# ReLU-squared attention and a gated feed-forward on one core: planner's order replaced by a written-out one, transposes in 64x64 tiles, score tiles in any two PSUM banks

## The chip, the cores and the metric

The kernel runs on one core of one Trainium2 chip. The metric is the time of one execution in device microseconds (us). Below, PE is TensorE (the matrix engine), PEld its weight loads, DVE is VectorE, ACT is ScalarE, POOL is GpSimd, which here only issues loads, and SP is SyncE, which issues stores and the transposes done by DMA. PSUM, where TensorE writes, has eight banks in this kernel.

## The reference

```python
batch, n_heads, seq, head_dim = (8, 12, 448, 64)
scores = scale * np.matmul(q, k.transpose(0, 1, 3, 2))
attn = np.maximum(scores, 0.0) ** 2 / S
attn_out = np.matmul(attn, v)
x = attn_out.transpose(0, 2, 1, 3).reshape(B * S, H * D)   # 3584 x 768
gate = np.maximum(x @ w_gate, 0.0)      # w_gate, w_val: 768 x 1536
val = x @ w_val
out = gate * val @ w_out                # w_out: 1536 x 768
```

Scores are passed through a ReLU and squared; there is no softmax. All inputs and the output are float32; the matrix products run in bf16.

## The kernel before, in words

**Units of work.** Heads are taken in quads: a pair (b, g) is batch b (0 to 7) and four of its 12 heads (g is 0 to 2), so there are 24 quads. A sequence of 448 is seven tiles of 64 rows.

For each quad, query and key are loaded (converted to bf16 by the load) into one tile `raw` of 128 partitions, queries in partitions 0 to 63 and keys in 64 to 127 (lines 468 to 488), and turned, so that the head's dimension lies along the partitions, into `qkT`. The first six quads are turned on TensorE: the three of batch 0 by `transpose_first` (L540, L547) in two parts, three of seven query tiles first; the three of batch 1 by `transpose_pe` (L588). The other 18 go through a copy (`perm`, L610 and L612) and a DMA transpose on SP's queue (`transpose_dma`).

Attention of a quad is seven score steps, each of four matmuls in 64x64 tiles (L686) into two neighbouring banks that begin at an even bank (0-1, 2-3, 4-5, 6-7), a ReLU out of PSUM (L697 on ACT, L699 on DVE), and a square in place (L709 on ACT, L711 on DVE). In batch 0 it is done in two passes over the queries, 192 columns first and then 256, with up to two key tiles in a step, four steps to a pass. Then 28 matmuls in 64x64 tiles form the product with v ("PV", L728) in a pair of banks, and a copy (L744 on ACT, L746 on DVE) puts it into `xT`, the input of the feed-forward.

The feed-forward of batches 0 and 1 is plain (`gv_plain`, L793): six matmuls for a block of 128 columns of w_gate, six for w_val, a ReLU on ACT (L801), a product on DVE (L803). Batch 0's first six blocks are done in two parts of 192 and 256 columns. From batch 2 on, two batches at a time are multiplied by a seven-product scheme of Strassen's kind (`gv_strassen`, L902), and the output layer (`out_both`, L1017) likewise for every two batches; these need sums of weights that DVE makes once (L820 to L839), copies of partial products out of PSUM (`snapshot`, L849 to L855), and additions on DVE (L930 to L968, L1007).

**What sets the order.** Nothing is executed on creation: every piece is an `Op` with the engines that may run it, what it depends on, which buffers it takes (`alloc`) and which it reads. Three lists hold TensorE's operations (attention, and `ffn`), the operations of the other engines (`others`) and POOL's loads. `plan` (L244) then walks through modelled time: TensorE's two lines are merged by the string `PE_ORDER`, the loads by `LOAD_ORDER`, and every other operation is given to the engine on which it would end first, with a small lead or lag from the string `AHEAD`. The `Planner` (L64) holds the modelled times, picks the buffer that comes free first, and, up to a modelled 32 us, puts filler matmuls (L1171, on constant data, read by nobody) in where TensorE would idle. The order that results is fixed when the kernel is built: on the chip each engine runs its own queue in that order and waits at each instruction for what it depends on.

A transpose on TensorE is a matmul of the data with the identity. In `transpose_pe` one instruction takes 128 partitions (query and key tile together) into 64 output partitions, 28 for a quad:

```python
for j in range(2):
    for t in range(NT):
        for h2 in range(2):
            nc.tensor.transpose(ps_b[64 * h2:64 * h2 + 64, ps2.idx + j, t * 128:(t + 1) * 128],
                                st.raw()[:, 2 * j + h2, t, :], ident)
```

The page writes the tiling as 128*64 there, and as 64*64 at scores and PV.

Of the kernel before, what the change touches and what calls it, by code (L numbers as in the profile page):

```python
# [15 lines left out]
class Res:  # L16


    def __init__(self, n):
        self.free = {i: 0.0 for i in range(n)}  # L20
        self.by = {}

    def at(self, i):

        t, op = self.free[i], self.by.get(i)
        return t if op is None else max(t, op.end + Planner.LATE[1])


class Buf:


    def __init__(self, res, among=None, width=1):
        self.res, self.width = res, width
        self.among = among if among is not None else sorted(res.free)
        self.readers, self.last, self.idx = 0, 0.0, None

    def pick(self, now=0.0):

        best = None
        for i in self.among:  # L40
            if all(i + w in self.res.free for w in range(self.width)):
                t = max(self.res.at(i + w) for w in range(self.width))
                if best is None or max(t, now) < max(best[0], now):
                    best = (t, i)
        return best


class Op:


    def __init__(self, engs, emit, deps=(), alloc=(), reads=(), mode=None, grp=None):
        self.engs, self.emit = engs, emit
        self.deps, self.alloc, self.reads = list(deps), list(alloc), list(reads)
        self.mode, self.grp = mode, grp
# [4 lines left out]
        self.start = self.end = self.eng = None  # L59
        for b in self.reads:  # L60
            b.readers += 1


class Planner:  # L64
    NOUT = 8
    SWITCH = 0.1
    BIAS = 0.2
    MARGIN = 1.5
    LATE = (2.0, 1.0, 0.3)
    TO_LOAD, LOADED = 2.35, 0.95  # L70
    TO_TURN, TURNED, TURN = 1.7, 0.8, 3.65
    ISSUE = 0.28
    TO_HW = 1.9
    COLD = 4.6, 1.6
    FILL_FROM = 0.4
    FILL_COLD = 5.5
    FILL_UNTIL = 32.0
    FILL_MARGIN = 0.1
    GV_ORDER = '1256734'
    OUT_ORDER = 'ab1cd572364'  # L80
    END_ORDER = ('517364', '523')
    BUFFERS = (3, 11, 3, 4, 4, 4, 3)
    PV_PAIRS = (0, 0)
    JOIN = True
    TWO_QUEUES = True
    SPLIT = False
    MERGE = False
    URGENT = {'sh': -0.5, 'perm': 0.5}
    YIELD = {'sq': 0.1, 'sh': 0.1}
    PV_AT_0 = 0  # L90
    QT = 3
    PART = 6
    PV_AT = (1, 1)
    T_AT = (1, 1)
    MORE_UNTIL = 6
    BY_PE = 6
    ORDER = 'LV610ab2c3x4oy5rzqp'

    def __init__(self, banks):
        self.banks = banks  # L100
        self.t = {"POOL": 1.25, "DVE": 0.85, "ACT": 0.74, "SP": 0.74}
        self.ops = []
        self.mode = None
        self.dma_t = 0.0
        self.queues = [], []
        self.loads = []

    def free_at(self, bank):
        return self.banks.free.get(bank, 1e9)

    def now(self, op):
        return self.t.get("PE", 0.0) if "PE" in op.engs else 0.0

    def ready(self, op):
        r = 0.0
        for d in op.deps:
            if d.end is None:
                return None
            if d.eng != "PE" or "PE" not in op.engs:
                r = max(r, d.end + (self.LATE[0] if d.xbar else self.LATE[2] if d.load else 0.0))  # L120
        for b in op.alloc:
            p = b.pick(self.now(op))
            if p is None:
                return None
            r = max(r, p[0])
        return r

    def best(self, op):
        r = self.ready(op)
        if r is None:  # L130
            return None
        c = None
        for e, (occ, busy) in op.engs.items():
            if e in ("DVE", "ACT"):
                r = max([r] + [d.end + self.MARGIN for d in op.deps if d.load and not d.hw])
            s = max(r, self.t.get(e, 0.0))
            if e == "PE" and op.mode != self.mode:
                s = max(r, self.t.get(e, 0.0) + self.SWITCH)
            f = s + busy + (self.BIAS if e == "DVE" and len(op.engs) > 1 else 0.0)
            if c is None or f < c[0]:  # L140
                c = (f, s, e)
        return c[1], c[2], r

    def rates(self, a, b):

        if not (a and b):
            return 1.0, 1.0
        share = a[0][0].share
        return 1.0 - share, share

    def flow(self, a, b, t, until):
        while t < until and (a or b):
            rates = self.rates(a, b)
            d = min([q[0][1] / r for q, r in zip((a, b), rates) if q] + [until - t])
            t += d
            for q, r, post in zip((a, b), rates, (self.LOADED, self.TURNED)):
                if q:
                    q[0][1] -= d * r
                    if q[0][1] < 1e-6:
                        q.pop(0)[0].end = t + post  # L160
        return t

    def transfer(self, queue, op, arrival, work):


        self.dma_t = max(self.flow(*self.queues, self.dma_t, arrival), arrival, self.dma_t)
        self.queues[queue].append([op, work])
        self.flow(*([list(x) for x in q] for q in self.queues), self.dma_t, 1e9)

    def commit(self, op, s, e):  # L170
        assert op.behind is None or op.behind.start is not None
        op.start, op.eng = s, e
        occ, busy = op.engs[e]
        if e == "PE" and s < self.COLD[0] and op.kind != "fill":
            occ, busy = occ * self.COLD[1], busy * self.COLD[1]
        now = self.now(op)
        self.t[e] = s + occ
        op.end = s + busy
        if e == "PE":
            self.mode = op.mode  # L180
        if op.hw:
            self.transfer(0, op, s + self.TO_HW, op.load)
        elif op.load:
            self.loads.append(op)
            self.transfer(0, op, s + (op.to or self.TO_LOAD), op.load)
        elif op.xbar:
            self.transfer(1, op, s + self.TO_TURN, self.TURN)
        else:
            op.end += op.land
        for b in op.alloc:  # L190
            t, b.idx = b.pick(now)
            assert t <= s + 1e-6
            for w in range(b.width):
                del b.res.free[b.idx + w]
                b.res.by.pop(b.idx + w, None)
            b.last = op.end
        for b in op.reads:
            b.readers -= 1
            b.last = max(b.last, op.end + (self.LATE[1] if op.land or op.xbar else 0.0))
            if b.readers == 0:  # L200
                for w in range(b.width):
                    b.res.free[b.idx + w] = b.last
                    if op.xbar:
                        b.res.by[b.idx + w] = op
        self.ops.append(op)
# [3 lines left out]
PE_ORDER = (  # L209
    'aaaccdabaabcbdafjabbaebbbaacdfhafcBBADDaabbabgaZLBKMBAccabaGCFFFCFFdagbaJJebjHHbbaAEFaadEcaaGBCBAAggcbaAFLDGFA'  # L210
    'PGGbaaCCCACgfcccBEbbaGEEDACedcccCCbbaDAfgAbbacBDCaaAAAhccbCCbaBCAaAadBeAabacBJbaDBACBDGcBFAAFAACBHAAGBAFBBCBAA'
    'BDfaAADaaCCAAcBBABaaABBAacbabDAGDAEABBCAIEAEACABAAcACbaAACAGAabbBABaaBCADAecbEACAaAFebaBACEAabEEFAfaBFgaCAabdA'
    'CbbaGBAdeCBecdCAaaaAAAABaebaAEKADBAQCBADADABAAAbaDBAbbBDAAACacFBAaabFBACCGCCABcbaCDBAADEbbaEABCAIBBAdIAAbdHFAA'
    'CaaDACCCaJACBABCBBfbaBABaccAACADbaAAAAadaaICAcaAAaaABAaabaBBbaaCEIACaFKBAAJABBAACABAAABCBBBACBCDCBAABAAAADADHC'
    'BDCBICHABCFBHACAFEBEHBABCAEGBBDBBDCCECAAAGBABBABBBCGEAABBCBCCBABBABBBA'
)
LOAD_ORDER = (
    'aaaaaafcbaakaacaaedbbbthbcabkacccefhbdiggaggaacddaaeebfdbecaccacabfdebcgagbaaeabhabddeaacejejafacacaammkbddbbf'
    'dacabba'
)  # L220
AHEAD = (
    'llmmmmmokormnnqmompmmmhjklmmnmipkpololmiqoqmkllqqmomnhllolkigjnnliqpkqgqhhhpoogrknspsnhshlookqpdonnfpqionrfqtn'
    'vnquafpyepllvskpmjquaslaoutinvmhcfqgyorlobnoqtvjgjlhcelpookkqilpkbselllhiclmsvapkwpqjjrogngkwmkmdcanruprtcgmtj'
    'srnqgtsopdunjkjkdkjrmrkrjnnrwisoqkkiknlllnqknpqrknfjokmiolpnfsxqlpdjnmglirqjjpnpkiiiloilpjpqosmionomrknpneelrm'
# [19 lines left out]
def plan(first, att, ffn, others, pool, still, filler, banks):  # L244
# [5 lines left out]
    pe = []  # L250
# [1034 lines left out]
```

## Time and profile before

| | |
|---|---|
| runs of the kernel, us | 402.48, 404.31, 405.04 |
| median, us | 404.31 |
| span of the profiled execution, us | 402.3 |
| granted TensorE clock, mean | 0.990 |
| DVE / ACT / POOL busy, us | 326.1 / 274.0 / 75.7 |
| first feed-forward matmul (L793) starts, us | 27.53 |
| last matmul's end (L1017), us | 398.2 |

The page gives no time of the profiled execution other than its span. "Span" runs from the first instruction to the last. A row such as `0.50 PE ps L686 x8` in the chain says that eight matmuls of line 686, writing `ps`, took 0.50 us of the chain of work that ended last. In the table of windows, the columns are the window, its length, the busy us and instructions of PE, PEld, DVE, ACT and POOL, the granted clock (1.00 is full), the share of the DMA engines (which goes over 1 where packets overlap) and GB/s. A timeline row gives start, length from first start to last end, engine, line, operation, tile written and read, tiling, shape and number, and the idle time ahead.

### The profile page before, as it was taken

The page shows a single profiled execution, that of the slowest core. Times are in us where ns is not written, and L with a number is a line of the kernel's source. Part 1 is how long each engine was busy: PE and PEld are TensorE (multiplying, and loading weights), DVE is VectorE, ACT ScalarE, POOL GpSimd, SP SyncE. Part 2 cuts the span into 40 slices and gives each one's busy share as a digit, 9 for nine tenths or more (in the row PEclk, how much of TensorE's full clock was granted, in tenths as well). Part 3 has the DMA queues.
Part 4 walks back from the last instruction along what each step waited for, and adds up shares of the span by engine and source line. Part 5 has one row for each costly group of instructions (what it writes and reads, how often), then busy time and mean ns, then how long its engine had stood idle before and what let it go on. Part 6 is the DMA issues. An engine that isn't in the chain of part 4 may idle for free.

```text
span 402.3 us, 8737 instructions
## 1 busy us (share of the span) xinstructions
PE 393.8 (98%) x3472; PEld 210.1 (52%) x3472; DVE 326.1 (81%) x568; ACT 274.0 (68%) x399; POOL 75.7 (19%) x121
## 2 busy tenths in 40 slices
PE   6999999999999999999999999999999999999995
PEld 3567745454455554444455554444555555555563
DVE  5688788999989879969988989888789967758662
ACT  3697786477979728969879868878788843333221
POOL 7946441020430110311030221300100000000000
PEclk9799999999999999999999999999999999999999
DMA  8999999948988995193698796682224320000245
GB/s 121 192 198 199 201 193 183 147 48 136 124 144 171 162 116 115 26 145 56 84 141 153 152 131 129 82 92 47 46 37 99 80 59 2 0 0 2 59 118 139
DMA packets 77337, 43.54 MB, mean 108 GB/s; under 512 B 40688, under 2 KB 77296, under 8 KB 77296
## 3 DMA queue, kind: packets, MB, share of 16 engines
q0 software_dynamic: 34640, 23.50, 43.1%
q1 hardware_dynamic: 42192, 18.98, 26.5%
q8 instruction: 27, 0.44, 0.5%
q10 hardware_dynamic: 464, 0.49, 0.4%
q14 instruction: 14, 0.11, 0.1%
HBM read 47.19 MB, written 11.01 MB: 145 GB/s over the span
## 4 chain that ended last, share of the span: by engine, by line
PE 95%; DMA 1%; DVE 1%; POOL 0%; issue 0%; ACT 0%; POOLq 0%
PE ps L902 36%; PE ps L1017 25%; PE ps L793 14%; PE ps L686 10%; PE ps L728 8%; DMA gvT<-in_q_dram 1%; PE ps L1171 1%; PE ps L540 1%; PE ps L588 1%; DVE at L711 1%; POOL gvT L404 0%; DVE at L699 0%; DVE qkT L515 0%; DVE f L853 0%; ACT xT L744 0%
## 5 line engine op out<-in xcount | busy, mean ns | idle before, releaser
L697 ACT ACTIVATE at<-ps 128x896 bf16<-128x896 f32 (+4 forms) x116 | 103.2, 906 | 22.6 <-PE ps L686 21.8
L849 ACT COPY f<-ps 128x448 f32<-128x448 f32 x99 | 52.1, 532 | 45.8 <-PE ps L902 34.2
L709 ACT ACTIVATE at<-at 128x896 bf16<-128x896 bf16 (+1 forms) x72 | 67.0, 947 | 2.0 <-DVE at L699 1.2
L711 DVE TENSOR_TENSOR at<-at 128x896 bf16<-128x896 bf16 (+4 forms) x99 | 58.9, 607 | 9.2 <-ACT at L697 8.1
L699 DVE TENSOR_SCALAR at<-ps 128x896 bf16<-128x896 f32 (+4 forms) x55 | 58.4, 1064 | 6.9 <-PE ps L686 6.2
L404 POOL DMA_DIRECT2D vv<-in_v_dram x44 | 26.7, 611 | 165.5 <-PE ps L686 152.5
L686 PE MATMUL ps<-qkT 64*64 64x448 bf16 (+2 forms) x756 | 51.5, 342 | 1.0 <-ACT xT L744 0.3
L902 PE MATMUL ps<-xT,gvT 128*128 128x448 bf16 x216 | 50.9, 353 | 0.0
L902 PE MATMUL ps<-sx,wv 128*128 128x448 bf16 x216 | 50.6, 353 | 0.1
L902 PE MATMUL ps<-xT,wg 128*128 128x448 bf16 x216 | 49.7, 353 | 0.0
L902 PEld LDWEIGHTS <-gvT 128*128 128x128 bf16 x324 | 30.7, 98 | 30.5 <-issue 3.2
L1017 PEld LDWEIGHTS <-sh 128*128 128x128 bf16 x312 | 29.5, 98 | 22.9 <-issue 3.6
L1017 PEld LDWEIGHTS <-hT 128*128 128x128 bf16 x270 | 25.3, 98 | 20.5 <-issue 4.5
L1017 PE MATMUL ps<-wo,hT 128*128 128x384 bf16 x192 | 35.6, 327 | 0.0
L686 PEld LDWEIGHTS <-qkT 64*64 64x64 bf16 x756 | 19.5, 106 | 27.5 <-issue 22.4
L728 PE MATMUL ps<-at,vv 64*64 64x448 bf16 (+2 forms) x700 | 33.4, 327 | 0.0
L1007 DVE SCALAR_TENSOR_TENSOR o<-ps,f 128x384 f32<-128x384 f32 x41 | 22.5, 554 | 12.1 <-PE ps L1017 7.2
L902 PEld LDWEIGHTS <-wv 128*128 128x128 bf16 x216 | 20.6, 98 | 21.0 <-issue 2.8
L793 PE MATMUL ps<-xT,wv 128*128 128x448 bf16 (+2 forms) x180 | 31.3, 316 | 0.0
L902 PEld LDWEIGHTS <-wg 128*128 128x128 bf16 x216 | 20.6, 98 | 19.9 <-issue 1.7
L851 ACT ACTIVATE f<-ps 128x384 f32<-128x384 f32 x37 | 18.2, 491 | 18.6 <-PE ps L1017 18.3
L793 PE MATMUL ps<-xT,wg 128*128 128x448 bf16 (+2 forms) x180 | 30.6, 315 | 0.0
(72 smaller groups left out, 495.5 us busy)
## 6 DMA issues: line engine op xcount, KB each, us to landing
out_dram<-o SPq DMA_DIRECT2D x108, 96.0 KB, 2.2
vv<-in_v_dram POOLq DMA_DIRECT2D x44, 112.0 KB, 5.1
raw<-in_k_dram POOLq DMA_DIRECT2D x18, 224.0 KB, 5.4
raw<-in_q_dram POOLq DMA_DIRECT2D x18, 224.0 KB, 6.0
wo<-in_moe_w_out_dram POOLq DMA_DIRECT2D x4, 576.0 KB, 16.7
wg<-in_moe_w_gate_dram POOLq DMA_DIRECT2D x5, 384.0 KB, 9.9
wv<-in_moe_w_val_dram POOLq DMA_DIRECT2D x5, 384.0 KB, 10.6
gvT<-in_k_dram POOLq DMA_DIRECT2D x5, 224.0 KB, 6.3
```

Of the source, the lines that this page charges most:

```text
L404: op = Op({"POOL": (0.5 + 0.0004 * n_desc,) * 2}, lambda: nc.gpsimd.dma_start(out=dst(), in_=src), deps=deps, alloc=alloc)
L686: nc.tensor.matmul(banks()[64 * j:64 * j + 64, z, h2], lhsT=self.k_of(j, h2, k), rhs=self.q_of(j, h2), start=True, stop=True)
L697: nc.scalar.activation(self.at_of(i, m), banks(), AF.Relu)
L699: nc.vector.tensor_scalar_max(self.at_of(i, m), banks(), 0.0)
L709: nc.scalar.activation(a, a, AF.Square)
L711: nc.vector.tensor_tensor(a, a, a, ALU.mult)
L728: nc.tensor.matmul(ps[64 * h2:64 * h2 + 64, ps2.idx + j, :n], lhsT=st.v_of(j, h2, c), rhs=self.at_of(c)[64 * j:64 * j + 64, 0, h2], start= ...
L793: nc.tensor.matmul(ps[:, pb.idx, z * n:(z + 1) * n], lhsT=w[:, kd, fc], rhs=xT_t[xbuf[b].idx][:, kd, cols], start=(kd == 0), stop=(kd == K ...
L849: nc.scalar.copy(dst, src)
L902: nc.tensor.matmul(ps[:, pb.idx, :S], lhsT=w(g)[:, fc], rhs=rhs, start=start and g == 0, stop=stop and g == KH - 1, skip_group_check=True)
L1007: op = Op({"DVE": V384}, lambda: nc.vector.scalar_tensor_tensor(o_t[ob.idx], ps[:, pb.idx, :OH], float(out_scale), f_t[fb.idx][:, :OH], AL ...
L1017: nc.tensor.matmul(ps[:, pb.idx, :OH], lhsT=lhs(kf), rhs=rhs(kf), start=start and kf == 0, stop=kf == FH - 1, skip_group_check=True)
```

## The change

The planner, its constants and its three strings go. In their place stands one string, `PLAN`, and a function `replay` that reads it: for each operation a number (two characters to the base 64, in the order of the lists passed at the end of the kernel), its engine if it may run on more than one, and the number of every buffer it takes; the number 4095 stands for filler, with bank, count and width.

```diff
+PLAN = (
+    '9r9p9nQ19o++7B6OQ2Q3Q5Q4QA09t9qQ80000Q7021++64609u0Q69s039w1012QB++536G9v00B3400D7020A613A31++235GA700451Q9A'
...
+)
+def replay(ops, filler):
+    text = iter(PLAN)
+    def number(n=1):
+        v = 0
+        for _ in range(n):
+            v = 64 * v + DIGITS.index(next(text))
+        return v
...
+        i = number(2)
...
+        if i == FILL:
+            filler(number(), number(), number(2))
+            continue
+        op = ops[i]
+        op.eng = list(op.engs)[number() if len(op.engs) > 1 else 0]
         for b in op.alloc:
+            b.idx = (number(), number()) if b.apart else number()
+        op.emit()
...
-    for op in plan(first, att, ffn, others, pool_ops, still_op, filler, r_ps):
-        op.emit()
+    replay([*sum(first, []), *att, *[o for o, _ in ffn], *others, *pool_ops], filler)
```

A pair of banks for scores or PV may now be any two; reads and writes step from one to the other:

```diff
-        return Buf(r_ps, among if among is not None else PAIRS, width=2)
+        return Buf(r_ps, width=2, apart=True)
+    def both(pair, src=None):
+        i, j = sorted(pair.idx)
+        return (ps if src is None else src)[:, i:j + 1:j - i, :]
```

All transposes on TensorE take 64x64 tiles, a query tile (a = 0) and a key tile (a = 1) each by itself and into a bank of its own. In `transpose_pe` that is 56 instructions, a alternating:

```diff
+    def turn(bank_of, st, a, slots, js=(0, 1), shift=0):
+        for t in slots:
+            for j in js:
+                for h2 in range(2):
+                    pb, c = bank_of(a, j)
+                    nc.tensor.transpose(ps_b[64 * h2:64 * h2 + 64, pb.idx, c + (t - shift) * P2:c + (t - shift + 1) * P2],
+                                        st.raw()[64 * a:64 * a + 64, 2 * j + h2, t, :],
+                                        ident[64 * a:64 * a + 64, 64 * a:64 * a + 64])
...
         def emit():
-            for j in range(2):
-                for t in range(NT):
-                    for h2 in range(2):
-                        nc.tensor.transpose(ps_b[64 * h2:64 * h2 + 64, ps2.idx + j, t * 128:(t + 1) * 128],
-                                            st.raw()[:, 2 * j + h2, t, :], ident)
+            for t in range(NT):
+                for a in range(2):
+                    turn(lambda a, j: (pbs[a], j * S), st, a, (t,))
```

In `transpose_first` a quad's keys are turned by two operations of 14 instructions, each with its own copy of 448 columns; they wait for the keys alone. Its early queries are turned by one operation of 12 (for the first quad two of 6), with one copy of 384 columns, and its late queries by one of 16 with a copy of 512, as before. Before, an early operation turned keys and queries together, with copies of 384 or 640 columns.

What `PLAN` holds of the start, in the order of each queue (S a score step, "b g / first column . step"; K, Q, L the turns of keys, early and late queries; fill as count x columns):

```
PE   fill 11x408; K00.0; Q00.0; fill 4x384; Q00.1; K00.1; fill 3x400; S00/0.1 .3 .0; fill 3x336; K01.0;
     fill 5x376; K02.0; S00/0.2; K01.1; Q01; K02.1; fill 3x304; S01/0.3 .0 .2; fill 5x408; Q02; S01/0.1; L00;
     fill 2x440; S02/0.3 .1; PV00/0; S02/0.0 .2; L01; S00/192.3; fill 2x320; S00/192.2; L02; PV01/0;
     S02/192.3; S00/192.0 .1; PV02/0; S02/192.1; S01/192.0; gate 0, 3; fill 2x416; gate 1; S01/192.2; PV00/192;
     S02/192.2 .0; value 0, 1; S01/192.1 .3; value 3; gate 2; value 2; turn 10; PV02/192; PV01/192; S10.5 ...
ACT  Q00 copy; ReLU 00/0.1 .0; K01.0; ReLU 00/0.2; K02.1; ReLU 01/0.3 .2; square 01/0.3; ReLU 01/0.1; L00;
     ReLU 02/0.3; xT 00; ReLU 02/0.2 .0, 00/192.2 .3, 02/192.3, 00/192.0; xT 02; ReLU 02/192.1; gate 0;
     ReLU 01/192.0; gate 3, 1; ReLU 01/192.2, 02/192.2 .0, 01/192.3 .1; gate 2; square 01/192.3 ...
DVE  ... ReLU 01/0.0; square 01/0.0; Q02; squares 01/0.2 .1; ReLU 02/0.1; squares 02/0.3 .1 .2; L01; L02;
     square 02/0.0; xT 01; ReLU 00/192.1 ...
POOL keys 00 (two loads), 01, 02; early q 01; v 00; late q 01, 00; early q 02; v 00; late q 02; v 02;
     w_gate 0; v 02, 01, 01; w_val 0; w_gate 2-3; w_gate 1; w_val 1; w_val 2-3; q 10; k 10; w_gate 4-5 ...
```

In POOL's queue before, early query 01 stood ahead of keys 02.

More of the change, by code (lines that the diff above doesn't have):

```diff
@@ L19, in __init__ @@
     def __init__(self, n):
[L20 to L26, printed above, removed]
-class Buf:
[L32 to L45, printed above, removed]
+        self.n = n
+class Buf:
+    def __init__(self, res, width=1, apart=False):
+        self.res, self.width, self.apart = res, width, apart
+        self.idx = None
 class Op:
-    def __init__(self, engs, emit, deps=(), alloc=(), reads=(), mode=None, grp=None):
+    def __init__(self, engs, emit, deps=(), alloc=(), reads=(), mode=None):
         self.engs, self.emit = engs, emit
         self.deps, self.alloc, self.reads = list(deps), list(alloc), list(reads)
-        self.mode, self.grp = mode, grp
+        self.mode = mode
         self.load = self.land = self.share = 0.0
@@ L58, in __init__ @@
         self.xbar = 0
[L59 to L120, printed above, removed]
-        for b in op.alloc:
[L122 to L205, printed above, removed]
@@ new lines, in replay @@
+def replay(ops, filler):
[5 more added lines that the diff above has]
+        return v
+    left = set(range(len(ops)))
+    while True:
+        try:
+            i = number(2)
+        except StopIteration:
+            break
+        if i == FILL:
+            filler(number(), number(), number(2))
+            continue
+        left.remove(i)
+        op = ops[i]
+        op.eng = list(op.engs)[number() if len(op.engs) > 1 else 0]
+        for b in op.alloc:
+            b.idx = (number(), number()) if b.apart else number()
+        op.emit()
+    assert not left
@@ new lines, in transpose_first @@
+        for j in range(2):
+            deps = [st.k_ops[j] if two else st.k_ops[0], id_op] + keys[-1:]
+            keys.append(pe(lambda j=j: turn(lambda a, j: (kb[j], 0), st, 1, range(NT), (j,)), 0.22,
+                           deps=deps, alloc=[kb[j]] + ([st.qt_buf] if j == 0 else []), mode="64x64"))
+        cps = [copy_qk(keys[j], kb[j], lambda j=j: qkT_t[st.qt_buf.idx][:, 1, j, :], lambda j=j: ps_b[:, kb[j].idx, :S], K448)
+               for j in range(2)]
+        if two:
+            qs = []
+            for j in range(2):
+                qs.append(pe(lambda j=j: turn(lambda a, j: (qb, j * HALF), st, 0, range(QT), (j,)), 0.095,
+                             deps=[st.q_ops[j], id_op] + (keys[:1] if j == 0 else qs), alloc=[qb] if j == 0 else [], mode="64x64"))
+        else:
+            qs = [pe(lambda: turn(lambda a, j: (qb, j * HALF), st, 0, range(QT)), 0.19, deps=st.q_ops + [id_op, keys[0]],
+                     alloc=[qb], mode="64x64")]
@@ L575, in rest @@
             return op
-        return ops, rest
+        return [*keys, *qs], rest
     def transpose_pe(b, g):
@@ L643, in __init__ @@
             m = 512 // n
-            starts = [*range(0, QT, m), *range(QT, NT, m)] if (b, g, c0) == (0, 0, 0) else range(0, NT, m)
+            starts = range(0, NT, m)
             ends = [*starts[1:], NT]
@@ L1012, in evac_add, with out_mm @@
         return op
-    def out_mm(lhs, rhs, pb, start, deps, seg, alloc=(), reads=(), grp=None):
+    def out_mm(lhs, rhs, pb, start, deps, seg, alloc=(), reads=()):
         def emit():
@@ L1074, in out_both @@
         rest = None
-        if Planner.JOIN and b == B - 4:
+        if b == B - 4:
             keep()
@@ L1160, with filler @@
     others.extend([still_op, id_op])
-    def filler(us, cold):
-        pb = bank([7, 6, 5, 4, 3, 2, 1, 0])
-        total = int(us * (1200 if cold else 2400))
-        n = (total + S - 1) // S
-        width = max(64, total // n)
-        def emit():
-            for _ in range(n):
-                nc.tensor.matmul(ps[:, pb.idx, :width], lhsT=still[:, :128], rhs=still[:, :width], start=True, stop=True)
-        op = Op({"PE": (us, us)}, emit, deps=[still_op], alloc=[pb], reads=[pb])
-        op.kind = "fill"
-        return op
+    def filler(bank, n, width):
+        for _ in range(n):
+            nc.tensor.matmul(ps[:, bank, :width], lhsT=still[:, :128], rhs=still[:, :width], start=True, stop=True)
     for g in range(NQ):
```

336 lines of the change are left out of this document (135 added, 201 removed).

## The prediction

> **What bounds the kernel now.** I read the page first, then the chain that ended last in order of time, then the windows of the first 30 us, then the timeline of TensorE. The page:
>
> ```profile
> span 402.3 us, 8737 instructions
> PE 393.8 (98%) x3472; PEld 210.1 (52%) x3472; DVE 326.1 (81%) x568; ACT 274.0 (68%) x399; POOL 75.7 (19%) x121
> ...
> PE   6999999999999999999999999999999999999995
> ...
> PE 95%; DMA 1%; DVE 1%; POOL 0%; issue 0%; ACT 0%; POOLq 0%
> ```
>
> TensorE is busy in every slice but the first and the last, so what counts is what it is busy with. The chain shows it:
>
> ```profile
> 21.05 1.67 PE ps L1171 x9
> ...
> 27.60 2.58 PE ps L793 x30
> ...
> 30.63 0.90 PE ps L588 x28
> 31.53 1.75 PE ps L728 x56
> 33.30 0.59 ACT xT L744
> 33.94 4.75 PE ps L793 x42
> ...
> 155.00 0.50 PE ps L686 x8
> ...
> 239.41 0.64 DVE f L853
> ...
> 398.20 0.56 DVE o L1007
> ```
>
> L1171 is filler that nobody reads. The first feed-forward product (L793) starts only at 27.53 (27.60 in the chain); from there to 398.2, 370.6 us, TensorE works almost without a gap: the waits in the chain are 0.59 at 33.30 and 0.64 at 239.41. In that stretch only useful columns and turns between tilings cost time. A pure score step of 8 matmuls takes 0.50 where 8 x 448 columns in four tiles are 0.37, and six output matmuls take 1.08 after a score step against 0.97 elsewhere, so each visit to 64x64 tiles costs 0.13 + 0.11 = 0.24 us; there are 64 visits after 27.5, 15 us. The start is another matter:
>
> ```profile
> 9.00:12.00 3.00, 2.94 (x44) 1.70 (x44) 1.35 (x4) 1.87 (x3) 2.59 (x5) 0.50 1.38 189
> 12.00:15.00 3.00, 3.00 (x47) 1.75 (x44) 1.87 (x4) 1.21 (x2) 3.00 (x5) 0.50 1.32 199
> 18.00:21.00 3.00, 2.66 (x101) 2.04 (x94) 2.97 (x7) 2.92 (x6) 3.00 (x5) 1.00 1.62 190
> ```
>
> From 9 to 15 TensorE is "busy" at a granted clock of 0.50, on filler and transposes, while ACT is busy 3.08 of 6; from 18 on DVE (2.97 of 3) and ACT (2.92) are full. So the start is limited by how early ScalarE and VectorE get their score tiles.
>
> **The part that the plan settles.** The profiled span is 402.3, 0.2 below the fastest of the three runs and 2.0 below their median, 404.31; the page has no time outside the span, so I make the sum on the span and carry the 2.0. Decoding PLAN (two characters an operation, then engine and buffers) gives 1782 operations and 10 fills. Products, their columns and the score matmuls are those of before; 65 visits to 64x64 tiles follow the first product, against 64. So after the start the plan neither adds nor removes TensorE work: +0.24 at most.
>
> What moves is the start. Ahead of the first product, PLAN has the three first score passes with their PV and 7 of the 12 steps of the second pass; before had 24 score matmuls and one PV of the second pass more behind it, and spent time on filler at 20.98, 23.35, 24.83 and 26.76. I follow the queue that ends last, ScalarE's.
> (1) The second quad's query load is now one place later on POOL (a 224 KB key load goes ahead). It landed at 8.92; 224 KB at 189 GB/s is 1.2 us, so 10.1. Turn (0.2), VectorE copies (0.4 + 0.36), scores and key copies on ScalarE: ReLU from about 12.0.
> (2) From there ScalarE has, to the last xT copy: ReLU 4 x 0.81, 2 x 0.49, 2 x 1.03, 2 x 0.60, one square 0.47 (estimate, half of the 768 row's 0.85), one key/query copy 0.57 (estimate between 0.48 for 384 and 0.90 for 896 columns), 2 xT copies x 0.48: 9.5 us. First product at 21.6 if it is never starved.
> (3) On to the last square that PV needs: 6 x 1.03 + 0.60 ReLU, 4 gate ReLU x 0.33, one square 0.60: 8.7, to 30.2, then one PV of 28 x 256 columns, 0.75: 30.9.
> (4) TensorE alone from 21.6 to there: 8 short products x 0.52 (2.58/5), fill 0.35, 36 score matmuls 0.96, 3 PV 2.24, one turn 0.47, three visits 0.72: 8.9, to 30.5. It is no longer than ScalarE.
> (5) VectorE from 12.0 to its last square before the first PV copy: 2 x 0.96 + 6 x 0.55 + 0.35 + 3 copies 1.2: 6.8, to 18.8; it is not the last.
> At that point the new order has three short products more than before had at 33.94 (1.55) and three score steps less (0.69): it stands where before stood at 34.8. Unstarved, the gain is 34.8 - 30.9 = 3.9. In 18 to 30 before, ScalarE was busy 11.08 of 12 us (92%); at that share the 18.2 us take 19.7 and the point is at 32.4: gain 2.4. I take the middle, **-3.2**, as the new list alternates as tightly as the old one.
>
> Weights and loads: 17 loads stand ahead of and with the first value weights. In destination bytes 2496 KB have to flow; the windows had let 2.2 MB through by 15 us and 2.8 by 18, so they flow by 17 and land 1.6 later, as the query load did (754 KB had flowed at 7.3): 18.6, before 21.6. The block that the third product needs comes at 21.6: TensorE may wait some tenths there, and the fill before it covers that. If loads slip by 1 us, so does the start.
>
> **The turns.** 28 transposes of 128x64 (L588) become 56 of 64x64. The nearest rows:
>
> ```profile
> 16.96 0.69 PE L547 MATMUL ps<-ident,gvT 64*64 64x64 bf16 x32 [0.41 <-DVE at L699]
> 30.56 0.97 PE L588 MATMUL ps<-ident,gvT 128*64 128x128 bf16 x28
> ```
>
> The first row is in two column tiles of one row half: (0.69 - 0.19 for the last one's length) / 32 = 15.6 ns each. With both row halves alternating, as `turn` is called, columns would share four ways: 56 x 7.8 = 0.44. If the pitch of 15.6 is a floor per instruction, 56 take 0.87 and nothing is won on 0.90. Scores in four tiles do run at a quarter of their columns (28 PV matmuls 1.32 us), so I take 0.47: -0.43 each, one of three already counted, **-0.86**.
>
> TensorE: Matmul & The Clock Gate (the Trainium skill, section "Wait — 56ns, not 53.3ns?") says that start-to-start never drops below about 25 ns however short a matmul. By that, an estimate, 56 turns would take 1.4 us and the three cost 2.8 more than in my sum, 403.0. The trace's 15.6 ns in tiles is against it.
>
> **Smaller parts.** First turns: keys apart from queries, 14 + 14 + 12 + 16 turns a quad; at 15.6 ns 0.9, against 1.53 (at half clock) + 0.25; they lie beside the ReLU queue, counted in (1), and if that cover goes they gain. Copies at the start: two of 640 and one of 512 (1.40) become two of 448, one of 384, one of 512 (0.39 x 2 + 0.36 + 0.42 = 1.56): counted in the queues. Pairs of banks apart: 138 of 171 score tiles and 18 of 27 PV tiles are no old pair. No row shows an eviction over banks apart; from below, nothing is won after 30 us, where no wait of TensorE on a bank is shown, and at most the 0.8 us of such waits ahead of it; from above, as much as two single copies against one wide one (2 x 0.53 - 0.92 = 0.15 us), on engines with 19% and 32% idle. I take 0. Engines: ReLU 130 on ACT and 41 on DVE (116 and 55), squares 103 on DVE (99), 26 copies of partial products move to DVE (13): by the rows ACT loses about 6 us and DVE gains 3; neither fills. SP keeps stores and DMA transposes in one queue as before; the end is the same last product, addition (0.56) and store, 4.1 us. POOL's loads after the start wait on buffers as before (24 us the longest), hidden. The 0.64 wait at 239 goes; I let one of its size take its place. Sum: -3.2 - 0.86 = -4.1; 404.3 - 4.1 = **400.2**, span 398.2.
>
> **Rivals.**
> B, better: ScalarE never starved (-3.9), no wait in the middle (-0.64), turns -0.86: -5.4, 398.9. Against it: the 92%. For it: the list is free to put any ready eviction next. 0.20.
> C, the clock halves again. Before, it fell at 9 after a window with TensorE busy 1.75 of 3.00; the fills between 9 and 18 (17 matmuls, 6,352 columns, 2.6 us) would last twice as long; part hides under ScalarE, so between +0.9 (the one fill of 5 x 408 right ahead of scores) and +2.6: 402.0. For it: key loads still land at about 9. Against: new fills stand at 5 to 9. 0.12.
> D, a turn has a floor that the number of active tiles doesn't lower: at 15.6 ns nothing is won in three turns, +1.2: 401.4. For it: no row shows a shorter pitch. Against: the scores' and PV's four-way sharing. 0.15. TensorE: Matmul & The Clock Gate (the Trainium skill) has such a floor, as told above.
> E, the other side: the middle. Every score visit is preceded by an eviction in a fixed order; if VectorE is late by the 0.64 of the row at 239, TensorE waits, as nothing overtakes. Seven such waits use up 4.1 us; at 13 of the 65 visits, 8.3 us, 408.5. For it: DVE at 81%, with slices of 9. Against: only one such wait in 370 us of a like order. 0.08.
>
> **How the numbers follow.** The forecast, 0.45 (own range 399 to 401.6), is the likeliest. About 1% (4.0 us, 400.27) is what a measurement tells from no change. Half of the forecast and all of B lie below, 0.22 + 0.20, and C or D with a start as in B, 0.05: faster 0.47. Slower than 408.35 is half of E, 0.04, and C, D and part of E together, 0.01: 0.05. The rest, 0.48, is the same. Range: B's 398.9 with its queue 0.9 earlier, 398.0, to C with D's, 403.2; outside lie E and the edges.
>
> **What would show it.** First product near 22 instead of 27.53; ReLU from 12.0; the state of 34.8 at 30.9 to 32.4; turns of 56 in 0.44 to 0.6 us; granted clock 1.00 from 9 to 15; no wait over 0.7 after 35; the end 4.1 after the last matmul. It is wrong if the first product is after 25, or if TensorE's waits after 35 add to over 2 us.

## The result and the profile after

| | before | after |
|---|---|---|
| median of the compared runs, us | 403.97 (402.48 to 405.04, 4 runs) | 503.77 (501.47 to 507.35, 4 runs) |
| span of the profiled execution, us | 402.3 | 505.5 |
| granted TensorE clock, mean | 0.990 | 0.939 |
| first feed-forward product starts, us | 27.53 | 33.40 |

The ratio is 1.2485 (95% interval 1.2417 to 1.2554). The forecast was 400.2, and 398.0 to 403.2. Slower by over 1% had a chance of 0.05, on the strength of rival E, which ended at 408.5. So the sign, the size and the place were all missed, and both signs of being wrong that the prediction named have come: the first product is after 25, and TensorE's waits after 35 us add to far over 2 us.

Here and below, a run over 1.5% above the fastest of its kernel is counted among the runs but left out of the ratios and their intervals.

The page after, in the same lines as before:

```profile
span 505.5 us, 8969 instructions
PE 424.9 (84%) x3598; PEld 221.2 (44%) x3598; DVE 330.8 (65%) x581; ACT 271.9 (54%) x388; POOL 75.5 (15%) x121
...
PE   7767688995888869988866799868798989999996
...
PE 72%; ACT 14%; DVE 9%; DMA 2%; issue 2%; DVEq 0%; SPq 0%; ACTq 0%
```

ScalarE and VectorE do about the work of before (ACT 271.9 against 274.0, DVE 330.8 against 326.1), so their instructions got no dearer; the engines stand still more. TensorE is out of work for 505.5 - 424.9 = 80.6 us, before 8.5: that is 72 of the 103 us. The other 31 are TensorE's own busy time (424.9 against 393.8): by the lower clock 393.8 would become 415 (x 0.990 / 0.939, an estimate), and some 10 I can't assign. The row of 40 slices tells where: holes throughout, except in the last six slices. From 428.5 on no attention is left, and TensorE has no wait at all in that stretch.

What it waits for stands in the list of TensorE's waits, of which these are some (line waited in, who released it; us in total, times, longest). Before, the same list has none after 35 us.

```profile
PE ps L721 <- ACT at L516: 16.2, 16, 2.6
PE ps L506 <- ACT at L516: 16.1, 18, 2.2
PE ps L612 <- ACT at L516: 9.6, 8, 2.2
PE ps L506 <- DVE at L518: 6.3, 6, 2.1
PE ps L836 <- ACT at L516: 5.6, 6, 1.4
```

L516 and L518 are the ReLUs that empty a pair of score banks; L506 is the scores; L721, L612 and L836 are products of the feed-forward, each into one bank of its own. Some waits of a product on a ReLU are due, when it takes over a bank from it. But the list for all engines holds waits between instructions that share no data: an eviction (a copy or ReLU out of PSUM) on an eviction by the other engine, or a ReLU on a product of the feed-forward.

```profile
DVE at L518 <- ACT at L516: 14.9, 9, 3.7
...
ACT at L516 <- DVE at L518: 11.4, 6, 3.7
...
ACT at L516 <- PE ps L721: 10.2, 11, 2.1
```

One place shows the mechanism. Here is the timeline of TensorE and ScalarE from 243.6 to 248 us (start, length, engine, line; in brackets the idle time ahead and what ended it):

```profile
243.63 0.76 PE L506 MATMUL ps<-qkT 64*64 64x448 bf16 x12
...
244.23 0.92 ACT L516 ACTIVATE at<-ps 128x896 bf16<-128x896 f32 x1 [1.10 <-PE ps L506]
...
245.20 0.73 PE L721 MATMUL ps<-sx,wv 128*128 128x448 bf16 x3 [0.81 <-ACT at L516]
245.77 0.73 PE L721 MATMUL ps<-xT,gvT 128*128 128x448 bf16 x3
245.97 0.92 ACT L516 ACTIVATE at<-ps 128x896 bf16<-128x896 f32 x1 [0.82 <-PE ps L721]
...
246.94 1.30 PE L721 MATMUL ps<-xT,wg 128*128 128x448 bf16 x6 [0.44 <-ACT at L516]
```

Decoding PLAN for this place gives the banks. The three score steps write banks 4 and 1, 2 and 7, 5 and 0. The first ReLU reads 1 and 4. The product at 245.20 adds into bank 3, which this ReLU doesn't touch but which lies between 1 and 4, and it starts when the ReLU has ended (244.23 + 0.92 = 245.15). The second ReLU reads 2 and 7; ScalarE has been free since 245.15, and waits until the product in bank 3 is done (245.20 + 0.73 = 245.93). The product at 245.77 goes into bank 1, outside of 2 to 7, and runs beside this ReLU. The two products at 246.94 go into banks 4 and 2 and wait for its end (246.89); of these two only bank 2 is one that it reads.

This gives **theory 1**: a read that steps over banks, `ps[:, i:j + 1:j - i, :]`, is ordered against everything in the banks between, not only against its own two. 139 of the 198 pairs in PLAN are not neighbours. **Theory 2**: the written-out order is so tight that any delay spreads. **Theory 3**: the low clock at the start (0.80 up to 35 us) and the turns cost it.

### The profile page after: what moved, and what is told of

It reads as the page before. It is cut to its first block, busy times and chain, and to the rows that moved or that the text cites. A ratio compares the mean times of both kernels' runs of the same rounds, so it can differ in the third digit from the quotient of the medians.

```text
span 505.5 us, 8969 instructions
## 1 busy us (share of the span) xinstructions
PE 424.9 (84%) x3598; PEld 221.2 (44%) x3598; DVE 330.8 (65%) x581; ACT 271.9 (54%) x388; POOL 75.5 (15%) x121
## 3 DMA queue, kind: packets, MB, share of 16 engines
q1 hardware_dynamic: 42192, 18.98, 21.6%
## 4 chain that ended last, share of the span: by engine, by line
PE 72%; ACT 14%; DVE 9%; DMA 2%; issue 2%; DVEq 0%; SPq 0%; ACTq 0%
PE ps L721 27%; PE ps L836 17%; PE ps L612 12%; ACT at L516 12%; PE ps L506 7%; PE ps L547 6%; DVE at L518 4%; PE ps L981 2%; ACT xT L563 2%; DMA out_dram<-o 1%; PE ps L359 1%; DMA raw<-in_k_dram 1%; DVE xT L565 1%; DVE f L672 1%; DVE sh L919 1%
## 5 line engine op out<-in xcount | busy, mean ns | idle before, releaser
L516 ACT ACTIVATE at<-ps 128x896 bf16<-128x896 f32 (+4 forms) x130 | 116.0, 903 | 92.8 <-PE ps L506 20.2
L506 PE MATMUL ps<-qkT 64*64 64x448 bf16 (+2 forms) x756 | 57.6, 356 | 30.0 <-ACT at L516 16.1
L530 DVE TENSOR_TENSOR at<-at 128x896 bf16<-128x896 bf16 (+3 forms) x103 | 61.4, 611 | 26.7 <-ACT at L516 26.1
L668 ACT COPY f<-ps 128x448 f32<-128x448 f32 x89 | 46.9, 532 | 54.2 <-PE ps L721 37.3
L518 DVE TENSOR_SCALAR at<-ps 128x896 bf16<-128x896 f32 (+3 forms) x41 | 44.0, 1073 | 40.0 <-ACT at L516 14.9
L528 ACT ACTIVATE at<-at 128x896 bf16<-128x896 bf16 (+1 forms) x68 | 62.8, 938 | 3.7 <-DVE at L518 3.1
L721 PE MATMUL ps<-sx,wv 128*128 128x448 bf16 x216 | 53.6, 365 | 8.4 <-ACT at L516 7.8
L721 PE MATMUL ps<-xT,wg 128*128 128x448 bf16 x216 | 52.8, 372 | 4.9 <-ACT at L516 3.8
L721 PE MATMUL ps<-xT,gvT 128*128 128x448 bf16 x216 | 50.9, 353 | 1.7 <-DVE at L518 1.7
L506 PEld LDWEIGHTS <-qkT 64*64 64x64 bf16 x756 | 21.9, 110 | 62.8 <-issue 60.4
L721 PEld LDWEIGHTS <-gvT 128*128 128x128 bf16 x324 | 31.2, 98 | 37.5 <-issue 9.8
L612 PE MATMUL ps<-xT,wv 128*128 128x448 bf16 (+2 forms) x180 | 37.5, 360 | 7.0 <-ACT at L516 5.0
L836 PEld LDWEIGHTS <-sh 128*128 128x128 bf16 x312 | 29.9, 98 | 29.8 <-issue 11.5
L612 PE MATMUL ps<-xT,wg 128*128 128x448 bf16 (+2 forms) x180 | 35.4, 350 | 5.9 <-ACT at L516 4.6
L236 POOL DMA_DIRECT2D raw<-in_k_dram x18 | 11.3, 629 | 165.7 <-DVE perm L441 151.6
L836 PE MATMUL ps<-wo,hT 128*128 128x384 bf16 x192 | 35.8, 326 | 0.3 <-DVE at L518 0.2
L836 PEld LDWEIGHTS <-hT 128*128 128x128 bf16 x270 | 25.6, 98 | 23.5 <-issue 7.6
L721 PEld LDWEIGHTS <-wv 128*128 128x128 bf16 x216 | 21.1, 100 | 31.8 <-issue 15.3
L721 PEld LDWEIGHTS <-wg 128*128 128x128 bf16 x216 | 22.1, 103 | 28.4 <-issue 11.9
L836 PE MATMUL ps<-woT,sh 128*128 128x384 bf16 x156 | 30.2, 333 | 2.6 <-ACT at L516 2.1
```

The lines of the kernel that those rows point to most:

```text
L236: op = Op({"POOL": (0.5 + 0.0004 * n_desc,) * 2}, lambda: nc.gpsimd.dma_start(out=dst(), in_=src), deps=deps, alloc=alloc)
L506: nc.tensor.matmul(banks()[64 * j:64 * j + 64, z, h2], lhsT=self.k_of(j, h2, k), rhs=self.q_of(j, h2), start=True, stop=True)
L516: nc.scalar.activation(self.at_of(i, m), banks(), AF.Relu)
L518: nc.vector.tensor_scalar_max(self.at_of(i, m), banks(), 0.0)
L528: nc.scalar.activation(a, a, AF.Square)
L530: nc.vector.tensor_tensor(a, a, a, ALU.mult)
```

## Experiments on the pairs of banks

**1. The same order, neighbouring banks.** PLAN keeps every operation, engine, buffer and fill; only the numbers of the banks change, so that all 198 pairs are neighbours. At the place above:

```diff
-score steps: banks (4, 1), (2, 7), (5, 0);  products: 3, 4, 2
+score steps: banks (6, 7), (0, 1), (2, 3);  products: 5, 7, 0
```

> The changed kernel with the same order, engines and fills; only PSUM banks are numbered anew, so that the two banks of every pair are neighbours (the free one that suits is taken, at the same places of the order). Theory 1, a stepped eviction of two banks apart is held to touch all banks between, so ReLU and PV copies wait for products in those and the products wait for them: nearly all of the 100 us goes, 396 to 406 us, TensorE waits under 10 us after 35 us. Theory 2, the written-out order itself is too thin and waits pile up: still 480 to 510. Theory 3, the half clock at the start and turns: 485 to 500.

Measured: 407.37 us (404.81 to 409.71, 9 runs), 1.4 above the upper end that theory 1 expected; to before (404.02) the ratio is 1.0079 (1.0046 to 1.0112). 96 of the 100 us are gone with the digits of the banks, so theories 2 and 3 can't hold more than the other 3.4. The two kinds of wait without shared data that are shown above are no longer in the list. The page of this kernel:

```profile
span 403.0 us, 8972 instructions
PE 390.7 (97%) x3598; PEld 207.4 (51%) x3598; DVE 327.8 (81%) x581; ACT 266.5 (66%) x388; POOL 75.9 (19%) x121
```

TensorE's busy time is back below that of before (393.8), and the granted clock was 1.00 in this execution: the 31 us of longer busy time went with the holes.

**2 and 3. Only the banks apart, in the kernel before.** The order, the engines and all else are those of before; the eight banks are renamed, so that every pair is four banks apart (0-4, 1-5, 2-6, 3-7), or two (0-2, 1-3, 4-6, 5-7):

```diff
+BANK = (0, 4, 1, 5, 2, 6, 3, 7)        # in the third experiment (0, 2, 1, 3, 4, 6, 5, 7)
+STEP = BANK[1] - BANK[0]
...
-                return ps[:, ps2.idx:ps2.idx + 2, :]...
+                return ps[:, BANK[ps2.idx]:BANK[ps2.idx + 1] + 1:STEP, :]...
```

> The kernel before, same order and same buffers; only the physical bank of each number is changed, so that the pairs 0-1, 2-3, 4-5, 6-7 become 0-4, 1-5, 2-6, 3-7. Theory 1 (all banks between are held): every one of 198 pair evictions spans five banks, over half of PSUM: slower than 460 us, TensorE waiting on ReLUs in the middle. Theory 2 (the order): no change, 402 to 406. An eviction itself, if reading apart costs nothing, stays at 0.91 us for 896 columns on ACT.

> As the run with pairs four apart, but pairs 0-2, 1-3, 4-6, 5-7: a span of three banks. Theory 1 expects a smaller loss than with four apart, 415 to 470 us, as one bank between is held and not three. Theory 2 expects no change, 402 to 406.

Measured: 587.9 us, ratio 1.4546 (1.4476 to 1.4616), with pairs four apart, and 453.61 us, ratio 1.1223 (1.1169 to 1.1277), with pairs two apart, from two runs each. So the distance sets the price. By theory 1, 0-2 and 1-3 are in the way only of each other, while 0-4, 1-5, 2-6 and 3-7 all span banks 3 and 4, so that a read of one pair is ordered against the reads of all the others. The evictions themselves are no dearer. In before, 98 ReLUs of 128x896 on ACT (L697) take 917 ns each, with 17.4 us of idle time ahead of them. The same group in the changed kernel, and then in the one with pairs four apart (number | busy us, mean ns | idle time ahead, and what ended it):

```profile
L516 ACT ACTIVATE at<-ps 128x896 bf16<-128x896 f32 x110 | 99.5, 917 | 78.5 <-PE ps L547 14.3 <-PE ps L506 14.0 <-DVE at L518 11.4
```

```profile
L700 ACT ACTIVATE at<-ps 128x896 bf16<-128x896 f32 x98 | 89.5, 917 | 120.8 <-DVE at L702 34.6 <-PE ps L731 22.0 <-PE ps L689 20.5
```

It is 917 ns in all three; what grows is the idle time ahead (17.4, 78.5, 120.8 us), and what ends it is no longer the scores that are read (L506, L689) alone, but any product or eviction.

**4. The changed kernel with its own banks, each bank emptied by its own instruction.** This separates the stepped read from the mere distance of the banks:

```diff
+                far = abs(ps2.idx[0] - ps2.idx[1]) != 1
+                for part in (slice(0, 1), slice(1, 2)) if far else (slice(0, 2),):
...
-                    nc.scalar.activation(self.at_of(i, m), banks(), AF.Relu)
+                        nc.scalar.activation(self.at_of(i, m)[:, :, part], banks()[:, :, part], AF.Relu)
...
-                    nc.scalar.copy(dst, src)
+                        nc.scalar.copy(dst[:, part], src[:, part])
```

(and the same on VectorE)

> The changed kernel with its own order and its own banks, far apart as they are; only the ReLU and xT copy of a pair that is not two neighbours is issued as two instructions, one bank each. Theory 1 (what costs is the one stepped access, which is held against everything in the banks between): each instruction then names exactly its own bank, so the false waits go and the time falls from 503.8 to near that of the neighbouring banks, 405 to 415 us; the price is on ScalarE and VectorE, some 0.14 us for each of about 156 split evictions (2 x 0.53 against 0.92), 22 us over two engines that have more than that idle. Rival 1b (banks that lie apart cost in themselves, for example by which bank is written beside which is read): the time stays near 500 us.

Measured: 405.98 us (405.07 to 408.17, 10 runs), before 403.64, ratio 1.0061 (1.0029 to 1.0093). All waits of TensorE that its trace lists, over the whole span:

```profile
PE ps L549 <- issue: 2.8, 2, 1.8
PE ps L506 <- ACT o L674: 2.7, 1, 2.7
PE ps L985 <- DVE woT L978: 1.4, 1, 1.4
```

Not one wait on a ReLU is left, with the same banks as far apart as in the changed kernel. Rival 1b falls: the distance costs nothing that these runs show if each read names one bank. The price of splitting was overestimated: it was 139 evictions and not 156, and against experiment 1, ACT is busy 5.9 us more (272.4) and DVE 2.1 (329.9), not 22 together.

## Experiments on what became of the start

With the banks out of the way, the order still is 0.6 to 0.8% behind the kernel before, not 1% ahead as forecast. Experiment 1's first product starts at 21.91, forecast 21.6; but the point that before reaches at 34.8 and that was to be at 30.9 to 32.4 comes at 33.24. The largest waits of TensorE in that trace, over the whole span:

```profile
PE ps L505 <- ACT o L669: 3.1, 1, 3.1
PE ps L546 <- issue: 2.2, 2, 1.4
PE ps L980 <- DVE woT L973: 1.4, 1, 1.4
PE ps L505 <- issue: 0.6, 1, 0.6
```

There are two new things here (the 1.4 at L980 is the filler's wait, at the very beginning, for the constants that VectorE writes, in before too): gaps for which nothing in the profile is the releaser, 2.9 us in all ("issue"), and one wait of 3.1 us on an output copy.

The timeline of TensorE places the gaps (start, length, engine, line; idle time ahead in brackets):

```profile
14.39 0.22 PE L358 MATMUL ps<-ident,gvT 64*64 64x64 bf16 x3 [0.18 <-issue]
...
19.49 0.36 PE L546 MATMUL ps<-at,vv 64*64 64x192 bf16 x7 [0.80 <-issue]
...
25.69 0.63 PE L505 MATMUL ps<-qkT 64*64 64x256 bf16 x15 [0.56 <-issue]
...
31.88 1.36 PE L546 MATMUL ps<-at,vv 64*64 64x256 bf16 x41 [1.40 <-issue]
```

They split a run of like matmuls in the middle. Counting matmuls in the windows up to each gap gives 223, 351, 479 and 607: 128 apart, which with a weight load each are 256 instructions. So **theory A**: TensorE's instructions arrive in blocks of 256, and a block came late. In before, where only 464 matmuls had run by 30 us (here 607 by 30.45), TensorE shows no such gap. Transfers took a share of 1.26 of the DMA engines' time in the first 30 us, in before 1.25, so their load alone doesn't make the difference.

The trace shows the blocks themselves. This kernel's page lists a transfer queue of the kind "instruction" (packets, MB, share):

```profile
q8 instruction: 28, 0.46, 0.5%
```

Each of the 28 packets holds 16,384 bytes, one for 257 of the 7196 matmuls and weight loads; the kernels with 3514 matmuls have 27. By the times of the packets in the trace, those of the start end at 12.88, 18.06, 24.48 and 30.51 us, and TensorE goes on at 14.39, 19.49, 25.69 and 31.88, 1.2 to 1.5 us behind each. Why they come no sooner isn't shown.

The Trainium skill says the same of the blocks: Runtime: NRT & Kernel Launch, section "Instruction fetch mechanics", has each engine fetch instructions ahead in blocks of 256, through a DMA queue of its own, at a cost that is "mostly hidden". The count agrees; hidden it was not, with up to 1.40 us a block here.

**5. The kernel before with the new turns alone** (56 transposes of 64x64 in batch 1's three quads):

```diff
-            for j in range(2):
-                for t in range(NT):
+            for t in range(NT):
+                for a in range(2):
...
-                            nc.tensor.transpose(ps_b[64 * h2:64 * h2 + 64, ps2.idx + j, t * 128:(t + 1) * 128],
-                                                st.raw()[:, 2 * j + h2, t, :], ident)
+                            nc.tensor.transpose(ps_b[64 * h2:64 * h2 + 64, ps2.idx + a, j * S + t * P2:j * S + (t + 1) * P2],
+                                                st.raw()[64 * a:64 * a + 64, 2 * j + h2, t, :],
+                                                ident[64 * a:64 * a + 64, 64 * a:64 * a + 64])
```

> The kernel before with one part of the change: the three quads of batch 1 are turned by 56 transposes in 64x64 tiles with the halves alternating, in place of 28 in 128x64; banks and order as before (the planner still reckons the old time). If four tiles share, 0.45 us for 56 and up to 1.3 us less in all, 402.5 to 404; if a turn has a floor of 15.6 ns, no change; if 25 ns, 1.5 us more.

Measured: 406.32 us (404.94 to 411.16, 12 runs), ratio 1.0061 (1.0031 to 1.0092). That is slower, where 402.5 to 404 was expected, though 56 turns take 0.67 from first start to last end at 28.06 where 28 took 0.97. In its profiled execution (408.96, above the median) the trace has one gap of 1.6 us without a releaser and a wait of 2.7 us for a load of v at 140.8. The gap comes after 605 matmuls and not 607; a packet of instructions ends at 32.81, and TensorE goes on at 34.21, 1.4 us behind it as above. That fits theory A, by which the gap could use up the gain of the shorter turns; the wait for v was not followed further.

**6. Neighbouring banks, and batch 1's turns as 28 of 128x64 again** (the reverse of the diff above).

> The order with neighbouring banks (407.4 us), and batch 1's three quads turned with 28 transposes of 128x64 again. In that kernel TensorE stood without any releaser after its 223rd, 351st, 479th and 607th matmul (0.22, 0.80, 0.56, 1.40 us), 128 matmuls apart; the fourth time in a PV, at 30.5 us. Theory A (TensorE runs out of delivered instructions, in blocks of 128 matmuls with their weight loads): the first three gaps stay; the fourth comes again after the 607th matmul, now 28 matmuls later in the order, so in another product than that PV, and is smaller or gone because fewer instructions were drained; time 407.4 + 3 x 0.45 for slower turns - 0 to 1.4 = 407 to 408.8, more likely within 0.3% of 407.4 than above it. Rival B (the gap belongs to the PV and what it reads): it stays at the PV, at 30.5 us, and the time rises by 1.3 to 408.7.

Measured: 405.03 us (402.72 to 408.03, 12 runs), ratio to before 1.0041 (1.0003 to 1.0079). That is less than either account expected (407 and 408.7). In the profiled execution the gaps are those after 351 and 479 matmuls (1.1 and 0.6); the fourth is gone, which theory A allowed, and so is the first, which it had said would stay. A gap that is gone shows no place; experiment 8 does.

**7. Neighbouring banks, one output copy later.** The wait of 3.1 us, with what stood around it in experiment 1:

```profile
134.38 0.49 ACT L669 ACTIVATE o<-ps 128x384 f32<-128x384 f32 x1 [3.50 <-DMA out_dram<-o]
134.77 1.72 ACT L515 ACTIVATE at<-ps 128x896 bf16<-128x896 f32 x2
134.92 0.38 PE L505 MATMUL ps<-qkT 64*64 64x448 bf16 x4 [3.07 <-ACT o L669]
```

The copy needs one of four `o` buffers, whose store was still on its way; behind it in ScalarE's queue stand two ReLUs of finished scores, and TensorE's next score step needs the bank that the copy empties. The edit moves the copy behind the two ReLUs and that score step behind three products:

```diff
-PE   S32.3, S32.1, S32.6; out p6; product 1, 2       ACT  output copy; ReLU 32.3, 32.1; copy of p6; ReLU 32.6
+PE   S32.3, S32.1; out p6; product 1, 2; S32.6       ACT  ReLU 32.3, 32.1; copy of p6; output copy; ReLU 32.6
```

> The order with neighbouring banks (407.4 us), with one output copy on ScalarE, the one that stood 3.5 us at 131 to 134.4 for a buffer whose store was still on its way, put behind two ReLUs, and the score step that takes its bank put behind three products. If that wait is what TensorE's only gap after 35 us comes from (3.07 us, the score step waiting for the bank), the gap goes and the time falls by 2.5 to 3.1 us, to 404.3 to 405; one more visit to 64x64 tiles costs 0.24 of it. Rival: the store is late because loads share the transfer engines, so the next copy or its buffer waits instead, and less than 1 us is won: 406.4 to 407.4.

Measured: 403.22 us (401.42 to 408.18, 12 runs), ratio 0.9987 (0.995 to 1.0025), and so below the 404.3 to 405 expected; TensorE's wait on this copy is 0.2. The gap is closed and no like wait took its place: by the two ratios, each to the kernel before measured beside it, 0.9% or 3.7 us less than experiment 1, about the 3.1.

**8. Both edits.**

> Both of the last two edits together. If they add: 403.5 to 405 us, between the kernel before (404.0) and 1 us below; it would then be shown that the new order is worth about what the old one is, once its banks are neighbours and its one output wait is out, and that the 5 us won at the start are not all kept. Rival: the granted clock dips that seven of nine runs of the neighbouring-banks kernel had (0.985 to 0.996) come again, and it stays at 405 to 407.

Measured: 402.41 us (401.73 to 402.98, 12 runs), ratio 0.996 (0.9933 to 0.9987): the lowest median of all these kernels, 0.4% below the one before and below the 403.5 to 405 expected. Its timeline has the four gaps again:

```profile
14.90 0.22 PE L358 MATMUL ps<-ident,gvT 64*64 64x64 bf16 x3 [0.89 <-issue]
...
32.34 0.62 PE L549 MATMUL ps<-at,vv 64*64 64x256 bf16 x13 [0.15 <-issue]
```

They come after 223, 351, 479 and 607 matmuls, as in experiment 1. Two PV products of 28 matmuls stand there in a row. The fourth gap now leaves 13 matmuls of the two, where it left 41: it has moved from the first product to the second, by exactly the 28 matmuls fewer that the turn takes. So the gap belongs to a count of instructions and not to what is multiplied, and rival B falls; it shrank from 1.40 to 0.15, and the sum from 2.9 to 2.4 us. Here too TensorE goes on 1.2 to 1.6 us behind the packets, which end at 13.66, 18.23, 24.94 and 30.78.

## Why the prediction was wrong, step by step

- **Pairs of banks apart ("I take 0", between -0.8 us and 0.15 an eviction): this step failed.** The price was looked for in the eviction itself, where it is indeed nothing (917 ns before and after). It is in what the read is ordered against: TensorE waits for reads that pass over its bank, and readers wait for it and for each other. That was 96 of 100 us. A bound from two copies against one wide one could not see this: the question was how many pairs can still be in use at once. The page PSUM — Partial Sum Buffer (the Trainium skill, section "PSUM bank collisions raise a hardware error") says that the chip itself doesn't stall engines that meet in a bank, and that software must keep them apart, bank by bank. That fits waits written into the program for more banks than needed, and experiment 4 agrees: 405.98 with the same banks, each read naming its own.
- **"After the start the plan neither adds nor removes TensorE work": right, and not enough.** Busy time with neighbouring banks is 390.7 (before 393.8). Work that is the same doesn't make waits the same. Rival E had the right side; its place, VectorE 0.64 late in 13 visits, was wrong, and its size by 95 us. Its 0.64 was also misread: the chain's rows of 0.59 at 33.30 and 0.64 at 239.41 are copies on other engines beside which TensorE's timeline shows work, with stops of 0.04 us (33.90 to 33.94) and 0.13 us (239.96 to 240.09).
- **First product at 21.6 to 22: right once the banks are neighbours** (21.91); the changed kernel had it at 33.40. In part that is luck: the chain of experiment 1 holds 1.0 us of gaps ahead of it that the sum didn't have.
- **The point of 34.8 at 30.9 to 32.4: 33.24, a gain of 1.6 instead of 3.2.** Ahead of it TensorE stood 2.9 us waiting for no one, and all four gaps lie on the chain that ended last. Without them it would be at 30.3 (an estimate), near the 30.9 that the sum gave for a queue never starved. The supply of instructions was not among the terms, and the plan's quick start, with 607 matmuls by 30.45, is what uses it up.
- **Turns, 56 in 0.44, taken as 0.47: right.** In experiment 1 the product behind them starts 0.47 after the first of them (29.38 to 29.85), in experiment 8, with 28, it is 0.90 (29.90 to 30.80). In the changed kernel:

```profile
60.49 0.62 PE L359 MATMUL ps<-ident,gvT 64*64 64x64 bf16 x54
```

- **One of 0.64 in the middle, "I let one of its size take its place": 3.1.** The output copy waited for a store that took 7.0 us to land, where loads and transposes were in flight; the prediction let this queue stand ("as before").
- **Clock (rival C).** In the changed kernel it was 0.80 up to 35 us, among the holes. In experiment 1's profile it is 1.00 from the start. In its nine runs it is 0.985 to 1.0, the slowest run having the lowest; why it dips in some runs was not found. In experiment 8 it is 0.997 to 1.0 in all 12.
- **The end** came 4.5 us after the last matmul in experiment 1 (forecast 4.1): one more wait of 1.7 for an `o` buffer ahead of the last sum.

Of the forecast 4.1 us, experiment 8 keeps 1.2. What remains open: the program's own list of waits was not read, so that the order over the banks between is made when the program is built, and not by the chip, is inferred from experiment 4 and from semaphore events in the traces (a semaphore is a counter that one engine counts up and another waits for; the product at 245.20 does carry a wait for ScalarE's, but the trace doesn't keep for which count); further, how much of the difference between experiments 1 and 6, and 7 and 8, is the turns (their intervals overlap), and what made the before-kernel with short turns slower apart from the one gap.

## What to carry to other kernels

When a change lets one access span several buffers, ask not what the access costs but what else lies inside the range from its first to its last byte, and how many such ranges can be open at once; if they must lie apart, read each by an instruction of its own. A wait between two instructions that share no data, in the list of waits, is the sign. And a faster start must also be fed: look for gaps without a releaser at equal counts of instructions before blaming the products around them.

## What the runs showed of the chip

- Transposes of 64x64 over all four tiles follow one another every 8.0 ns ((0.62 - 0.19) / 54), half the pitch of 15.6 that the kernel before had shown in two. TensorE: Matmul & The Clock Gate (the Trainium skill, section "Wait — 56ns, not 53.3ns?") has a floor of about 25 ns from start to start; for small tiles side by side this trace disagrees.
- TensorE can run short of instructions: gaps of 0.15 to 1.8 us, always after the 223rd, 351st, 479th or 607th matmul, in the five kernels with the new start and neighbouring or split reads, each ending 1.2 to 1.6 us behind a packet of 16,384 bytes on the queue of instructions.
- Holes can cost clock as well, but need not: the mean granted clock was 0.939 where TensorE stood idle for 80.6 us (the changed kernel), 0.912 for 135.5 us (pairs four apart) and 0.999 for 44.0 us (pairs two apart). At 0.939 alone its work takes some 21 us longer (an estimate). They lengthen its busy time without the clock too: it was 407.6 us with pairs two apart, against 393.8 before at 0.990; the cause of that was not found.
